# Seeding a PSUM bank by a copy so that the matmuls do the adding, in a seven-product feed-forward kernel

## The chip, the cores and the metric

The kernel runs on one core of a Trainium2 chip. The metric is device time in microseconds of one launch; the median of the runs counts, and a profile comes from one further execution. The core's engines are named as the profile names them: PE (matmuls), PEld (its weight loads), DVE, ACT and POOL, and SP, which here only issues DMAs. Each engine takes its instructions in the order in which they stand in its own program, and waits in place when an operand is not ready.

## The reference

One transformer block on 2048 tokens of width 1024: a layer norm with scale and shift from a condition vector, causal attention with a running memory in 4 segments and 32 heads, a residual, a second norm, and a gated feed-forward part of inner width 3584. The change lies in the last part:

```python
def _B_ref(x, w_gate, w_up, w_down):
    return (_gelu(x @ w_gate) * (x @ w_up)) @ w_down
...
    h = _layernorm(x, axis=-1) * (1 + cb) + sb
    x = x + gb * _B_ref(h, B_w_gate, B_w_up, B_w_down)
```

All of it is in 32-bit floats. The kernel keeps that precision by writing each operand as a high part and a low part and taking three matmuls (high-high, high-low, low-high) for each product of two 128-row tiles.

## The kernel before, in words

**The seven products.** A matrix product of 2 by 2 blocks is formed with seven block products instead of eight. The products are numbered 1 to 7, and each result block is a sum of several of them. Product 1 is the base: it is a term of all four result blocks. Products 6, 7, 5, 4 and 3 are added on top of it, and block (1,1) is product 1 plus product 2.

**Order of the work.** Attention fills the first 920 us. The projection behind it (`project`, with its DVE addition at L777) has 32 output tiles, and the last four of them, `block(3, 1)`, end at about 1125 us. Then comes the feed-forward part in three stages:

- `two(n)`, n = 0 to 13: products 1 and 2 of the outer scheme depend on the gate weights alone. They are formed here ahead of time for pairs of column chunks, with an inner scheme of seven. Index i = 1, 2 is the outer product, r the inner one, and each (i, r) is six matmuls of 128x512 (L1140). For n = 0 all r of i = 1 run before those of i = 2, and later the two alternate. `ended(i, r)` takes the bank of the product to SBUF: base r = 1 is copied by ACT to a tile `c` (L1150); for r = 6, 7, 4 DVE adds the bank `pb` and `c` (L1156); for r = 5, 3 DVE adds the bank `pc` to the result tile (L1158); r = 2 is taken from the bank `pa` by ACT (L1160) or DVE (L1162). For i = 2 POOL adds the result of i = 1 (`total`), and ACT applies the gelu (L1173). Both results go to DRAM (`st_d`).
- `gate_up(m)`, m = 0 to 55 (28 column chunks for two halves of the tokens): the outer products 6, 5, 7, 3, 4 in this order, twelve matmuls each (L1372). 6, 7 and 4 add up in the bank `pb`, 5 and 3 in the bank `pc`. The base `c1` and the finished gate half `g1` come back from DRAM. After each product DVE adds: `u2 = pb + c1` (L1384), `u3 = pc + c1` (L1387), `u3 = pb + u3` (L1390), `u2 = pc + u2` (L1393), `h2 = pb + c1` (L1397). Then ACT applies the gelu to `h2` in place (L1398) and DVE multiplies (L1399).
- `down()`: the last product, with a scheme of seven over the whole of it (L1572). The change leaves its operations alone and gives its tiles other buffers.

**What sets the order.** All engines' instructions are written out in program order in this part, by Python generators that a `step()` after each product advances: cuts of operands into high and low (`cut`: ACT writes the high part at L925, DVE or POOL subtracts at L922), loads, and the norm of the last tokens. `a_first` is the generator that prepares the token operands `AA` of `two`; `summed` in it forms sums of blocks, with one subtraction on POOL in 128x256 halves between two DVE operations. It runs beside `block(3, 1)` and the first `two`. `norm_tiles` with the name "c" transposes the last 512 tokens' tiles through a PSUM bank (L269), and ACT (L277) and DVE (L275) take them out.

**PSUM.** There are eight banks: two of tag "mm" (`pa`, and the projection's `y`), five of tag "s" (`pb`, `pc`, and much else) and one of tag "o".

Of the kernel before, what the change touches and what calls it, by code (L numbers as in the profile page):

```python
# [19 lines left out]
P = 128  # L20
# [16 lines left out]
def block_kernel(ctx: ExitStack, tc: tile.TileContext, x, c, wmod, wq, wkv, wo, beta, wg, wu, wd, out):  # L37
# [212 lines left out]
    def norm_tiles(src, dst, segs, jscale, jshift, name, tiles=range(4), wait=0, get=raw_tile, more=[]):  # L250
# [12 lines left out]
        def turn(q, h):  # L263
            t, tok = xs[q], toks[q]
            ps = s_ps(f"tp{name}{tok}_{h}")
# [608 lines left out]
    ROUND = (1, 6, 2, 7, 5, 4, 3)  # L874
# [5 lines left out]
    def feed_forward():  # L880
# [8 lines left out]
        def place(n):  # L889
            r, i = n // 8, n // 4 % 2  # L890
            at = (0 if r in (0, 2) else 1) if i == 0 else 2 if r < 4 else 3
            return ffp[at], f"A{n}"
# [8 lines left out]
        def pair_tile(name, tag, bufs, dt=F32):  # L901
            return ffp[3].tile([P, 2, HM], dt, name=name, tag=tag, bufs=bufs)
# [62 lines left out]

        def put_two(i, r, c, src, eng):
# [16 lines left out]
        def a_early():  # L983
# [7 lines left out]
            for k, r in enumerate((1, 2)):  # L991
                for c in range(2):
                    put_two(1, r, c, ts[1, c][0][:, k], nc.vector)
                    yield

# [3 lines left out]
        def a_first():  # L999

            while not normed(0, 2):
                yield
            for c in range(2):
                ts[1, c].append(unit(1, c, 1, raw_tile))
            units(0, ra_tile)
            for _ in range(3):
# [3 lines left out]
            def summed(i, c, eng=nc.gpsimd):  # L1010
# [3 lines left out]
                diff(a21, a11, a21, eng)  # L1014
# [3 lines left out]
            def put(i, r, c):  # L1018
                if r == 1:
                    put_two(i, r, c, ts[i, c][0][:, 0], nc.vector)  # L1020
                    return
                src = sums[i, c]
                if r == 3:
                    nc.vector.tensor_sub(src[3], src[2], src[6])
                put_two(i, r, c, src[r], nc.gpsimd if c and r in (5, 4) else nc.vector)

            for c in range(2):
                summed(1, c)
                yield
            for r in (6, 7, 5, 4, 3):  # L1030
                for c in range(2):
                    put(1, r, c)
                    yield
            put(2, 1, 0)
            yield
            summed(2, 0)
            yield
            for r in ROUND[1:]:
                if r == 5:
                    while (2, 1) not in ts:  # L1040
                        yield
                put(2, r, 0)
                yield
            while not ff.get("half"):
                yield
            put(2, 1, 1)
            yield
            summed(2, 1, nc.vector)
            yield
            for r in ROUND[1:]:  # L1050
                put(2, r, 1)
                yield
# [25 lines left out]
        def seven(b11, b12, b21, b22, t1, t2_, put):  # L1078
# [5 lines left out]
            yield  # L1084
            yield
# [3 lines left out]
            diff(b12, b22, b12)  # L1089
            yield  # L1090
            put(7, b12, nc.vector)
            diff(t2_, b21, t2_)
            yield
            yield
            put(5, t1, nc.vector)
            yield
            put(4, t2_, nc.vector)
            yield
            put(3, b22, nc.vector)
# [21 lines left out]
        def two(n):  # L1121

            e, o = 2 * n, 2 * n + 1
            pa, pb, pc, c, out = {}, {}, {}, {}, {}

            def product(i, r):
# [4 lines left out]
                elif r == 6:  # L1131
                    pb[i] = s_ps(f"pb{n}_{i}")
# [4 lines left out]
                for k in range(2):  # L1137
                    at = (i - 1) * 2 * P + k * P
                    for a, b in ((0, 0), (0, 1), (1, 0)):
                        nc.tensor.matmul(ps, w[:, a, at:at + P], A["a", i, r, k][b],  # L1140
                                         start=(r in (1, 6, 5) and k == a == b == 0), stop=(k == 1 and a == 1),
# [4 lines left out]
            def ended(i, r):  # L1146
                if r == 1:
                    c[i] = c_tile(f"c{n}_{i}")
                    out[i] = [pair_tile(f"{'xy'[i - 1]}{n}_{q}", "Tg"[i - 1], 5 if i == 1 else 3) for q in range(2)]
                    nc.scalar.activation(c[i], pa[i], AF.Copy)  # L1150
                    return
                z = out[i]
                q, p = {6: (1, 0), 2: (0, 0), 7: (1, 1), 5: (1, 1), 4: (0, 1), 3: (1, 0)}[r]
                t = z[q][:, p]
                if r in (6, 7, 4):
                    nc.vector.tensor_add(t, pb[i], c[i])  # L1156
                elif r in (5, 3):
                    nc.vector.tensor_add(t, pc[i], t)  # L1158
                elif i == 1:
                    nc.scalar.activation(t, pa[i], AF.Copy)  # L1160
                else:
                    nc.vector.tensor_add(t, pa[i], out[1][q][:, p])  # L1162
                if r in (6, 7):
# [7 lines left out]
                if r != 2:  # L1171
                    total(t, t, out[1][q][:, p])
                later(2, lambda: nc.scalar.activation(t, t, AF.Gelu_apprx_tanh))  # L1173
                later(4, put)

            for i, r in [(i, r) for i in (1, 2) for r in ROUND] if n == 0 else [(i, r) for r in ROUND for i in (1, 2)]:
                product(i, r)
                if n == 0 and (i, r) == (1, 4):
                    ff["half"] = True
                if n == 0 and (i, r) == (1, 3):  # L1180
                    for q in (1, 2):
                        b_two_load(q)
                    sides.append([chain(wait_for(1), b_two(1)), 1, "b"])
                if n == NJ - 1 and (i, r) == (2, 4):
# [13 lines left out]
        def a_next(p):  # L1198
# [3 lines left out]
            T_tile = lambda n: pair_tile(n, "T", 5)  # L1202
            homes = [T_tile] * 3 + [ra_tile] * 2 + [raw_tile] * 2 + [T_tile] * 3 if p == 0 else (
# [11 lines left out]
            for _ in range(5 if p else 7):  # L1215
                load()
            yield
            for q, (i, b) in enumerate(todo):
                if q > p:
                    load()  # L1220
                if p == 0 and q == 7:
# [51 lines left out]
        def w_all():  # L1273
# [25 lines left out]
            def cuts(j):  # L1299
                (e, o), (t1, t2_, t4) = rows[j], sums[j]  # L1300
                for i, src in ((6, t2_), (7, e[:, L:]), (5, t1), (4, t4)):
                    t = pair_tile(f"T{j}_{i}", "T", 5, F32R)
# [53 lines left out]
        def gate_up(m):  # L1356
# [27 lines left out]
            nc.vector.tensor_add(u2, pb, c1)  # L1384
# [576 lines left out]
```

## Time and profile before

| what | us |
|---|---|
| median of 3 runs (lowest to highest) | 2721.28 (2719.34 to 2723.15) |
| the profiled execution, own time | 2725.75 |
| its span, first to last instruction | 2724.0 |
| PE busy with matmuls in it | 2672.9 |
| DVE, ACT, POOL busy | 1752.6, 1260.2, 1066.6 |
| PE busy with the matmuls of `gate_up` (L1372) | 766.0 |
| stretch of `two`, 1125.3 to 1417.0: length, PE busy | 291.7, 280.01 |
| stretch of `gate_up`, 1417.0 to 2186.0: length, PE busy | 769.0, 765.36 |

A row of the timeline gives start, duration, engine, line, operation, result and operands, how many instructions in a row were merged, and in brackets how long the engine had been idle before and what ended that. A row of a group gives, behind the bar, the busy time in us and the mean duration in ns. Matmuls overlap: a row of PE counts each from its start to a modelled end, so a mean of 390 ns stands beside a start every 228 ns. The granted clock of TensorE (PEclk) is given as a share of full speed.

### The profile page before, as it was taken

The page shows a single profiled execution, that of the slowest core. Times are in us where ns is not written, and L with a number is a line of the kernel's source. Part 1 is how long each engine was busy: PE and PEld are TensorE (multiplying, and loading weights), DVE is VectorE, ACT ScalarE, POOL GpSimd, SP SyncE. Part 2 cuts the span into 40 slices and gives each one's busy share as a digit, 9 for nine tenths or more (in the row PEclk, how much of TensorE's full clock was granted, in tenths as well). Part 3 has the DMA queues.
Part 4 walks back from the last instruction along what each step waited for, and adds up shares of the span by engine and source line. Part 5 has one row for each costly group of instructions (what it writes and reads, how often), then busy time and mean ns, then how long its engine had stood idle before and what let it go on. Part 6 is the DMA issues. An engine that isn't in the chain of part 4 may idle for free.

```text
span 2724.0 us, 42592 instructions
## 1 busy us (share of the span) xinstructions
PE 2672.9 (98%) x14068; PEld 2223.2 (82%) x14068; DVE 1752.6 (64%) x3747; ACT 1260.2 (46%) x2924; POOL 1066.6 (39%) x1644
## 2 busy tenths in 40 slices
PE   7999999999999999899999999999999999999999
PEld 6798888888888788678877888888888888888887
DVE  6676656776777745577776655566676654575456
ACT  6778777777777634354442222232222233233323
POOL 4233334433333532365667777645665300000000
PEclk9999999999999999999999999999999999999999
DMA  7355445435443567466779988789999896785563
GB/s 263 104 158 154 120 129 149 134 112 155 115 125 105 174 228 244 143 218 212 249 268 335 333 270 270 263 304 369 374 370 374 318 339 231 264 304 201 182 208 124
DMA packets 265644, 612.32 MB, mean 225 GB/s; under 512 B 26960, under 2 KB 51536, under 8 KB 265424
## 3 DMA queue, kind: packets, MB, share of 16 engines
q1 hardware_dynamic: 265424, 609.61, 67.3%
q8 instruction: 111, 1.82, 0.3%
q14 instruction: 109, 0.89, 0.1%
HBM read 371.48 MB, written 187.70 MB: 205 GB/s over the span
## 4 chain that ended last, share of the span: by engine, by line
PE 89%; DVE 3%; DMA 2%; issue 2%; ACT 1%; POOL 1%; SPq 0%; DVEq 0%; POOLq 0%; ACTq 0%
PE f L1372 27%; PE y L1572 19%; PE kv L395 9%; PE q L401 6%; PE y L773 5%; PE pb L1140 3%; PE S L607 3%; PE T L695 3%; PE O L707 3%; PE pa L1140 2%; PE pc L1140 2%; PE kT L514 2%; PE vT L514 2%; PE num L663 1%; PE M L646 1%
## 5 line engine op out<-in xcount | busy, mean ns | idle before, releaser
L1372 PE MATMUL f<-A,B 128*128 128x512 f32 x3360 | 766.0, 390 | 3.6 <-DVE c L1390 2.1
L1372 PEld LDWEIGHTS f<-A,B 128*128 128x128 f32 x3360 | 631.5, 188 | 137.6 <-issue 4.0
L1572 PE MATMUL y<-B,L 128*128 128x512 f32 x2352 | 533.8, 389 | 0.7 <-ACT L L925 0.3
L1572 PEld LDWEIGHTS y<-B,L 128*128 128x128 f32 x2352 | 441.4, 188 | 93.0 <-ACT L L925 0.8
L611 ACT ACTIVATE sj<-sj,mm 128x384 f32<-128x384 f32 (+3 forms) x512 | 281.1, 552 | 40.0 <-DVE mm L609 39.5
L698 POOL TENSOR_SCALAR_AFFINE_SELECT pt<-pt 128x128 f32<-128x128 f32 x512 | 166.6, 347 | 331.6 <-ACT pt L697 323.8
L609 DVE CUSTOM_DVE_ANT_0 sj<-S,mask 128x384 f32<-128x384 f32 (+3 forms) x512 | 228.2, 488 | 96.5 <-PE S L607 69.4
L697 ACT ACTIVATE pt<-T 128x256 f32<-128x256 f32 (+3 forms) x512 | 182.3, 442 | 132.0 <-PE T L695 125.5
L1398 ACT ACTIVATE g<-g 128x512 f32<-128x512 f32 x56 | 35.4, 632 | 414.9 <-DVE g L1397 414.9
L925 ACT ACTIVATE L<-X 128x512 fp32r<-128x512 f32 x168 | 105.8, 630 | 256.7 <-PE y L1572 162.7
L922 DVE TENSOR_TENSOR L<-X,L 128x512 fp32r<-128x512 f32 x168 | 115.9, 691 | 145.4 <-ACT L L925 145.4
L386 POOL TENSOR_TENSOR w<-r,w 128x256 fp32r<-128x256 f32 x180 | 133.8, 774 | 141.6 <-ACT w L380 141.6
L395 PE MATMUL kv<-w,hha 128*128 128x256 f32 x896 | 173.8, 284 | 2.2 <-DVE vx L413 2.2
L1286 POOL TENSOR_TENSOR rw<-rw,gbb 128x256 f32<-128x256 f32 x112 | 107.7, 996 | 153.8 <-DMA rw<-wd 119.8
L395 PEld LDWEIGHTS kv<-w,hha 128*128 128x128 f32 x896 | 143.9, 191 | 3.4 <-DVE vx L413 2.5
L1140 PE MATMUL pb<-AA,BB 128*128 128x512 f32 x504 | 128.1, 401 | 8.1 <-DVE x L1156 4.7
L773 PE MATMUL y<-wo,hho 128*128 128x512 f32 x384 | 128.9, 399 | 2.6 <-DVE xr L777 2.6
L395 PE MATMUL kv<-w,hla 128*128 128x256 f32 x448 | 126.6, 282 | 0.0
L1140 PEld LDWEIGHTS pb<-AA,BB 128*128 128x128 f32 x504 | 96.1, 193 | 31.9 <-DVE x L1156 5.9
L695 PE MATMUL T<-qs,ks 128*128 128x256 f32 (+3 forms) x512 | 105.7, 327 | 1.8 <-DVE ry L674 1.1
L607 PE MATMUL S<-ks,qs 96*128 96x384 f32 (+3 forms) x512 | 106.8, 329 | 0.3
L925 ACT ACTIVATE B<-t 128x512 fp32r<-128x512 f32 x84 | 49.7, 623 | 118.7 <-POOL t L922 118.7
(284 smaller groups left out, 5176.3 us busy)
## 6 DMA issues: line engine op xcount, KB each, us to landing
B<-wc_d SPq DMA_DIRECT2D x112, 512.0 KB, 4.2
cg<-st_d SPq DMA_DIRECT2D x112, 256.0 KB, 6.6
hid_d<-g SPq DMA_DIRECT2D x56, 512.0 KB, 4.5
wc_d<-T SPq DMA_DIRECT2D x56, 512.0 KB, 6.8
X<-hid_d SPq DMA_DIRECT2D x112, 256.0 KB, 4.8
bc_d<-B SPq DMA_DIRECT2D x54, 512.0 KB, 5.9
B<-bc_d SPq DMA_DIRECT2D x54, 512.0 KB, 7.4
wr<-gd_d SPq DMA_DIRECT2D x84, 256.0 KB, 4.0
```

Of the source, the lines that this page charges most:

```text
L395: nc.tensor.matmul(ps, b[:, sl], w[:, a], start=(kt == 0 and a == 0 and b is hi), stop=(kt == KT - 1 and a == 1), **kw)
L401: nc.tensor.matmul(ps, w[:, a], b, start=(kt == 0 and a == 0 and b is hi), stop=(kt == KT - 1 and a == 1), **kw)
L607: nc.tensor.matmul(ps[:, :nk], qs[:96, j, i * P:(i + 1) * P], ks[:96, j, :nk], start=True, stop=True)
L609: nc.vector.tensor_tensor_reduce(out=sj[:, :nv], in0=ps[:, :nv], in1=mask[:, L - nv:], scale=-1.0, scalar=3.4e38, op0=ALU.add, op1=ALU.min ...
L611: nc.scalar.activation(sj[:, :nv], sj[:, :nv], AF.Exp, bias=mm[:, j, i:i + 1], scale=-1.0, accum_out=ll[:, i, j:j + 1])
L695: nc.tensor.matmul(ps[:, :nn], ks[:, j, kc * P:(kc + 1) * P], qs[:, j, L - nn:], start=True, stop=True)
L697: nc.scalar.activation(pt, ps[:, nn - n:nn], AF.Exp)
L698: nc.gpsimd.affine_select(pt[:, :P], pt[:, :P], pattern=[[1, P]], compare_op=ALU.is_ge, fill=0.0, base=0, channel_multiplier=-1)
L773: nc.tensor.matmul(ps, b[:, i * P:(i + 1) * P], w[:, a, g % 2], start=(g == 0 and a == 0 and b is hi), stop=(g == G - 1 and a == 1))
L1140: nc.tensor.matmul(ps, w[:, a, at:at + P], A["a", i, r, k][b], start=(r in (1, 6, 5) and k == a == b == 0), stop=(k == 1 and a == 1), skip ...
L1372: nc.tensor.matmul(ps, B[m, i][:, a, kt * P:(kt + 1) * P], A[p, i, kt][b], start=(start and kt == 0 and a == 0 and b == 0), stop=(kt == 3 ...
L1572: nc.tensor.matmul(banks[t], ops[k][:, y, t * P:(t + 1) * P], B[slots[k]][:, x], start=(i not in (2, 4, 3) and j == 0 and x == 0 and y == ...
```

## The change

- **Base through PSUM.** In `two`, ACT copies the bank `pa` of product 1 into the bank `pb` instead of into an SBUF tile, and product 6 adds onto it. In `gate_up`, ACT copies `c1` from SBUF into the bank `pb` in front of product 6, which adds onto it. The sums with the base that DVE made are then in the bank: what was a DVE addition after products 6, 5 and 4 becomes an ACT copy out of the bank, or, for product 4 of `gate_up`, the gelu read straight from the bank. DVE keeps the additions after 7 and 3.
- **Order of the seven** in `two`: 1, 5, 6, 2, 7, 3, 4 instead of 1, 6, 2, 7, 5, 4, 3; the result of i = 1 is added to that of i = 2 by DVE, and POOL's additions fall away. The cuts of the weights follow the new order.
- **Banks that accumulate.** Five matmuls, one into each "s" bank, stand in front of the first `two`, so that later matmuls add in these banks. The transposes of the late norm ("c") move to the bank of tag "o", of which there is one.
- **Operands of `two`.** `summed` makes all its differences on DVE; i = 1 and i = 2 are prepared alike, both halves of i = 2 before the first `two` has ended; the low half of a cut is written one call later than its high half (`owed`, `settle`). Tiles of tag "T" (five buffers) are split into "T" (three) and "U" (two, in another pool), and the loads of `a_next` use them.

```diff
-            ps = s_ps(f"tp{name}{tok}_{h}")
+            ps = (o_ps if name == "c" else s_ps)(f"tp{name}{tok}_{h}")
...
-    ROUND = (1, 6, 2, 7, 5, 4, 3)
+    ROUND = (1, 5, 6, 2, 7, 3, 4)
...
-            cut(hl[0], hl[1], src, eng)
-            A["a", i, r, c] = hl
+            nc.scalar.activation(hl[0], src, AF.Copy)
+            settle()
+
+            def low():
+                each(eng.tensor_sub, eng, hl[1], src, f32(hl[0]))
+                A["a", i, r, c] = hl
+
+            owed.append(low)
...
-            def summed(i, c, eng=nc.gpsimd):
+            def summed(i, c):
                 (a11, a12), (a21, a22) = ((t[:, 0], t[:, 1]) for t in ts[i, c])
                 s1 = tmp_tile(f"s1_{i}_{c}")
                 nc.vector.tensor_add(s1, a21, a22)
-                diff(a21, a11, a21, eng)
+                nc.vector.tensor_sub(a21, a11, a21)
                 nc.vector.tensor_sub(a11, s1, a11)
...
             def ended(i, r):
                 if r == 1:
-                    c[i] = c_tile(f"c{n}_{i}")
-                    out[i] = [pair_tile(f"{'xy'[i - 1]}{n}_{q}", "Tg"[i - 1], 5 if i == 1 else 3) for q in range(2)]
-                    nc.scalar.activation(c[i], pa[i], AF.Copy)
+                    pb[i] = s_ps(f"pb{n}_{i}")
+                    nc.scalar.activation(pb[i], pa[i], AF.Copy)
                     return
...
-                if r in (6, 7, 4):
-                    nc.vector.tensor_add(t, pb[i], c[i])
-                elif r in (5, 3):
-                    nc.vector.tensor_add(t, pc[i], t)
+                base = out[1][q][:, p] if i == 2 else None
+                if r == 5:
+                    nc.scalar.activation(t, pc[i], AF.Copy)
+                elif r == 6:
+                    nc.scalar.activation(t, pb[i], AF.Copy)
+                elif r in (7, 3):
+                    nc.vector.tensor_add(t, (pb if r == 7 else pc)[i], t)
+                    if base is not None:
+                        nc.vector.tensor_add(t, t, base)
...
-            g = pair_tile(f"g{m}", "g", 3)
+            g = pair_tile(f"g{m}", "g")
             h1, h2_ = (g[:, q] for q in range(2))
-            product(pb, 6, True)
-            nc.vector.tensor_add(u2, pb, c1)
+            nc.scalar.activation(pb, c1, AF.Copy)
+            product(pb, 6, False)
+            nc.scalar.activation(u2, pb, AF.Copy)
             step()
             product(pc, 5, True)
-            nc.vector.tensor_add(u3, pc, c1)
+            nc.scalar.activation(u3, pc, AF.Copy)
             step()
             product(pb, 7, False)
             nc.vector.tensor_add(u3, pb, u3)
...
             product(pb, 4, False)
-            nc.vector.tensor_add(h2_, pb, c1)
-            nc.scalar.activation(h2_, h2_, AF.Gelu_apprx_tanh)
+            nc.scalar.activation(h2_, pb, AF.Gelu_apprx_tanh)
...
+        for q in range(5):
+            nc.tensor.matmul(s_ps(f"full{q}"), B["a", 0, 1][:, 0, :P], A["a", 1, 1, 0][0], start=True, stop=True)
```

**Order on ACT between `gate_up(4)` and `gate_up(5)`.** ACT's program before, from the gelu of m = 4 to that of m = 5. `g4` and `g5` are the result tiles of m = 4 and 5, and `B6_i` the cut weights of product i for m = 6:

```order
L1398 ACTIVATE g4_17922<-g4_17922 128x512 [waits DVE_49]
L925 ACTIVATE B6_6_18083<-t1_6_18053 128x512 [waits PE_49,DMAHW6_49,Activation_49,Pool_49]
L925 ACTIVATE B6_5_18095<-t0_6_18052 128x512 [waits PE_49,Activation_49]
L925 ACTIVATE B6_7_18106<-ru6_17911 128x512 [waits PE_49,DMAHW3_49,Activation_49,Pool_49]
L925 ACTIVATE B6_3_18117<-ru6_17911 128x512 [waits DMAHW4_49,PE_49,Activation_49]
L925 ACTIVATE B6_4_18138<-t1_6_18053 128x512 [waits PE_49,Activation_49,Pool_49]
L1398 ACTIVATE g5_18040<-g5_18040 128x512 [waits DVE_49]
```

The same place now; `f0_5` is the bank `pb` of m = 5, `f1_5` its bank `pc`, `cg5_0` the base loaded from DRAM, `c0_5` and `c1_5` the tiles u2 and u3:

```order
L1401 ACTIVATE g4_17845<-f0_4_17841 128x512 [waits PE_49]
L1386 ACTIVATE f0_5_17959<-cg5_0_17715 128x512 [waits DMAHW0_49]
L1388 ACTIVATE c0_5_17961<-f0_5_17959 128x512 [waits DVE_49,PE_49]
L1391 ACTIVATE c1_5_17962<-f1_5_17960 128x512 [waits DVE_49,PE_49]
L926 ACTIVATE B6_6_18007<-t1_6_17977 128x512 [waits DMAHW6_49,Activation_49,Pool_49]
L926 ACTIVATE B6_5_18019<-t0_6_17976 128x512 [waits Activation_49]
L926 ACTIVATE B6_7_18030<-ru6_17834 128x512 [waits DMAHW3_49,Activation_49,Pool_49]
L926 ACTIVATE B6_3_18041<-ru6_17834 128x512 [waits DMAHW4_49,DVE_49]
L926 ACTIVATE B6_4_18062<-t1_6_17977 128x512 [waits Activation_49,Pool_49]
L1401 ACTIVATE g5_17963<-f0_5_17959 128x512 [waits PE_49]
```

The gelu of m = 4 now reads the bank and waits for PE, and the copy that seeds the bank for m = 5 stands directly behind it. The cuts stand behind two copies that wait for products 6 and 5 of m = 5. On PE the first matmul into `f0_5` waits for ACT. So it is at all 55 borders between one m and the next.

**Order on DVE at the start of `block(3, 1)`.** DVE's program before, up to the addition that frees the bank of tile 0 of `block(3, 1)` (`y3_1_0`); `u1_0_0`, `u1_0_1` and so on are token tiles of i = 1, and `s1` is a sum of two:

```order
L1013 TENSOR_TENSOR s1_1_0_14617<-u1_0_1_14603 128x512 [waits DMAHW4_49,DMAHW3_49,DMAHW5_49,DMAHW0_49,Activation_49]
L1015 TENSOR_TENSOR u1_0_0_14293<-s1_1_0_14617,u1_0_0_14293 128x512 [waits DVE_49,Pool_49]
L1013 TENSOR_TENSOR s1_1_1_14628<-u1_1_1_14605 128x512 [waits DMAHW5_49,DMAHW2_49]
L1015 TENSOR_TENSOR u1_1_0_14295<-s1_1_1_14628,u1_1_0_14295 128x512 [waits DVE_49,Pool_49]
L922 TENSOR_TENSOR AA1_6_0_1_14634<-u1_0_0_14293,AA1_6_0_0_14633 128x512 [waits Activation_49]
L777 TENSOR_TENSOR xr2_14586<-y3_1_0_14596,xr2_14586 128x512 [waits PE_49]
```

The same place now:

```order
L1028 TENSOR_TENSOR s1_1_0_14621<-u1_0_1_14603 128x512 [waits DMAHW4_49,DMAHW3_49,DMAHW5_49,DMAHW0_49,Activation_49]
L1029 TENSOR_TENSOR u1_0_1_14603<-u1_0_0_14286,u1_0_1_14603 128x512 [waits DVE_49]
L1030 TENSOR_TENSOR u1_0_0_14286<-s1_1_0_14621,u1_0_0_14286 128x512 [waits DVE_49]
L1028 TENSOR_TENSOR s1_1_1_14631<-u1_1_1_14605 128x512 [waits DMAHW5_49,DMAHW2_49]
L1029 TENSOR_TENSOR u1_1_1_14605<-u1_1_0_14288,u1_1_1_14605 128x512 [waits DVE_49]
L1030 TENSOR_TENSOR u1_1_0_14288<-s1_1_1_14631,u1_1_0_14288 128x512 [waits DVE_49]
L777 TENSOR_TENSOR xr2_14586<-y3_1_0_14596,xr2_14586 128x512 [waits PE_49]
```

The addition L777 had five DVE operations ahead of it, two of which waited for POOL, and has six now, none of which does.

More of the change, by code (lines that the diff above doesn't have):

```diff
@@ L999, in a_first @@
         def a_first():
-            while not normed(0, 2):
+            while not normed(0, 2) or len(ffp) < 3:
                 yield
@@ L1170, in ended @@
                     return
-                if r != 2:
-                    total(t, t, out[1][q][:, p])
                 later(2, lambda: nc.scalar.activation(t, t, AF.Gelu_apprx_tanh))
-                later(4, put)
+                later(3, put)
+            if n == 0:
+                while ("a", 1, 4, 1) not in A:
+                    next(ff["first"])
+                b_two_load(1)
             for i, r in [(i, r) for i in (1, 2) for r in ROUND] if n == 0 else [(i, r) for r in ROUND for i in (1, 2)]:
@@ L1178, in two @@
                 if n == 0 and (i, r) == (1, 4):
[L1179 to L1184, printed above, removed]
+                    b_two_load(2)
+                    sides.append([b_two(1), 1, "b"])
+                if n == NJ - 1 and (i, r) == (2, 3):
                     for q in range(2):
```

112 lines of the change are left out of this document (52 added, 60 removed).

## The prediction

> **What bounds the kernel now.** I read the page first, then the waits of PE in the stretch that the change touches, then the granted clock around the long waits. From the page, PE's share, the costliest group and the gelu:
>
> ```profile
> PE 2672.9 (98%) x14068; PEld 2223.2 (82%) x14068; DVE 1752.6 (64%) x3747; ACT 1260.2 (46%) x2924; POOL 1066.6 (39%) x1644
> ...
> L1372 PE MATMUL f<-A,B 128*128 128x512 f32 x3360 | 766.0, 390 | 3.6 <-DVE c L1390 2.1
> ...
> L1398 ACT ACTIVATE g<-g 128x512 f32<-128x512 f32 x56 | 35.4, 632 | 414.9 <-DVE g L1397 414.9
> ```
>
> PE is busy for 98% of the span. In `gate_up` it was idle for 3.6 us in all, and a matmul took 766.0/3360 = 0.228 us of it. DVE and ACT have slack: ACT's gelus waited 414.9 us for DVE, and nobody waited for them. So work taken off DVE or ACT is worth only what PE now waits for. These are all waits of PE from 1103 to 2186 us (line, what it waited for, total, times, longest):
>
> ```profile
> PE pb L1140 <- DVE x L1156: 4.7, 3, 3.3
> PE pa L1140 <- DVE xr L777: 2.9, 1, 2.9
> PE y L773 <- DVE xr L777: 2.6, 1, 2.6
> PE pb L1140 <- DVE y L1156: 2.5, 4, 1.2
> PE f L1372 <- DVE c L1390: 2.1, 1, 2.1
> PE pc L1140 <- DVE y L1158: 1.8, 1, 1.8
> PE pa L1140 <- ACT c L1150: 1.7, 2, 1.1
> PE f L1372 <- ACT B L925: 0.7, 1, 0.7
> PE pb L1140 <- ACT AA L925: 0.7, 1, 0.7
> PE f L1372 <- DVE c L1384: 0.7, 2, 0.5
> PE pb L1140 <- DVE AA L922: 0.2, 1, 0.2
> ```
>
> They sum to 20.6 us. Some of these waits cost twice, because PE ran at half the granted clock behind them (each row: stretch, length, busy us of PE, PEld, DVE, ACT, POOL, then the clock):
>
> ```profile
> 1109.40:1112.80 3.40, 3.27 (x8) 2.59 (x9) 3.40 (x6) 2.66 (x6) 1.70 (x2) 0.50 0.27 98
> 1126.50:1129.90 3.40, 3.40 (x10) 2.66 (x9) 1.27 (x2) 1.63 (x3) 0.00 (x0) 0.50 0.42 153
> 1150.70:1154.10 3.40, 3.37 (x15) 2.80 (x16) 1.18 (x2) 0.73 (x2) 3.34 (x5) 1.00 0.00 0
> 1406.40:1413.20 6.80, 5.86 (x14) 4.57 (x15) 6.80 (x12) 4.40 (x9) 2.40 (x2) 0.50 0.75 267
> 1443.90:1447.30 3.40, 3.40 (x8) 2.65 (x9) 3.37 (x5) 0.00 (x0) 3.40 (x4) 0.50 1.03 349
> ```
>
> The four stretches at 0.50 follow the waits of 2.6, 2.9, 3.3 and 2.1 us. The 1.8 us wait (third row) was followed by a clock of 1.00. Half clock for 3.4 us costs 1.7 us, so the 17.0 us at 0.50 cost 8.5. All that the change can win on these waits is 20.6 + 8.5 = 29 us, 1.1% of the time.
>
> **The change part by part: the border of `gate_up`.** ACT's instructions are in fixed order. At each of the 55 borders the gelu of m now waits for PE's last matmul of product 4, the copy that seeds the bank of m + 1 stands behind that gelu, and PE's next matmul waits for the copy. Before, PE's next matmul opened an empty bank and waited for nothing. PE now stands still for: end of matmul to start of gelu, start of gelu to start of copy, the copy, and end of copy to matmul. Rows for each, an eviction by ACT in attention, an ACT pair and a base copy in `two`, and a restart of PE behind ACT:
>
> ```profile
> 529.97 0.39 PE L514 MATMUL vT<-hhh,w 128*128 128x512 f32 x1
> ```
>
> ```profile
> 530.39 0.60 ACT L543 ACTIVATE vt<-vT 128x512 f32<-128x512 f32 x1 [0.57 <-PE vT L514]
> ```
>
> ```profile
> 1127.48 0.60 ACT L1150 ACTIVATE c<-pa 128x512 f32<-128x512 f32 x1 [3.63 <-PE pa L1140]
> 1127.97 0.62 ACT L925 ACTIVATE AA<-s 128x512 fp32r<-128x512 f32 x1
> ```
>
> ```profile
> 1160.58 0.58 ACT L1150 ACTIVATE c<-pa 128x512 f32<-128x512 f32 x1
> ```
>
> ```profile
> 1161.21 1.65 PE L1140 MATMUL pa<-AA,BB 128*128 128x512 f32 x6 [0.60 <-ACT c L1150]
> 1162.70 1.52 PE L1140 MATMUL pb<-AA,BB 128*128 128x512 f32 x6
> ```
>
> - Matmul end 530.36 to ACT's start 530.39: 0.03.
> - A bank read by ACT to the next ACT instruction: 1127.97 − 1127.48 = 0.49.
> - The copy itself, SBUF to PSUM, is not in the trace. Its nearest rows are PSUM to SBUF, 0.58 (L1150); I take 0.58. Ends: 0.49 (the rate of issue above) and 0.63 (the gelu, SBUF to SBUF).
> - Copy's end 1161.16 to the matmul at 1161.21: 0.05.
> - The idle time is thus 0.03 + 0.49 + 0.58 + 0.05 = 1.15 us. The overlap of neighbouring matmuls, 0.390 − 0.228 = 0.16, is lost on top, and six matmuls after such a wait took 1.65 against 1.52, 0.13 more.
>
> Per border 1.15 + 0.16 + 0.13 = 1.44 us, and 55 × 1.44 = **+79.2 us**. With 0.49 for the copy and no slow restart it is 1.22, 67 us. With 0.63 and one more ACT instruction (0.49 to 0.53) at half of the borders it is about 1.76, 97 us. I see no row by which it could be nothing, since PE has no other work in its order between the two products.
>
> [...]
>
> **The rest of `gate_up`.** Three of DVE's seven operations per m become ACT's, or go. The evictions of 6 and 5 by ACT have cover: bank `pb` is next written by product 7, after twelve matmuls of product 5 (2.7 us), against 0.6 for the copy. ACT's cuts of weights now stand behind them. ACT's order at a border before:
>
> ```profile
> 1598.95 0.63 ACT L1398 ACTIVATE g<-g 128x512 f32<-128x512 f32 x1 [5.59 <-DVE g L1397]
> ...
> 1606.32 0.64 ACT L925 ACTIVATE B<-t 128x512 fp32r<-128x512 f32 x1 [4.65 <-POOL t L922]
> 1612.55 0.63 ACT L1398 ACTIVATE g<-g 128x512 f32<-128x512 f32 x1 [5.59 <-DVE g L1397]
> ```
>
> The last cut before a gelu waits for POOL and ended 5.6 us before the gelu; the eviction of 5 starts some 7 us after the gelu, so the cuts begin about 7 us later than now, and that last cut may come close to the gelu. I take 0, and make it a rival. PE's 2.1 us wait at 1443.83 stays: DVE's addition L1390 stood behind an operation that waited for a load, which the change does not touch:
>
> ```profile
> 1441.87 1.21 DVE L959 TENSOR_TENSOR m<-rm,rm 128x512 f32<-128x512 f32 x1 [4.10 <-DMA rm<-h_d]
> ```
>
> So 0, with a bound of −(2.1 + 1.7) = −3.8. The very first copy (m = 0) comes behind the end of `two`: +1.0, from 0 to 3 (the longest wait of that place now, 3.3).
>
> **`two`.** The waits on what the change takes off DVE and POOL are 4.7 + 2.5 + 1.8 + 1.7 = 10.7 us, and with half clock at 1406 (6.8/2 = 3.4) 14.1. Banks of 6 and 5 must still be emptied, by ACT, which has gelus and cuts in its order there, and DVE still adds to the bank sums of 7 and 3. I take −6, under half, between −14.1 and as much again as the waits now, +10.7. The copy from `pa` to `pb` costs nothing: product 5 of the same index, six matmuls and 1.52 us, lies between product 1 and product 6, against 0.03 + 0.58 + 0.05. If another ACT wait stood ahead of it, that is the +10.7.
>
> **`block(3, 1)` and the start of `two`.** DVE before:
>
> ```profile
> 1104.60 0.69 DVE L1015 TENSOR_TENSOR u<-s,u 128x512 f32<-128x512 f32 x1 [1.60 <-POOL u L922]
> ...
> 1107.58 0.69 DVE L1015 TENSOR_TENSOR u<-s,u 128x512 f32<-128x512 f32 x1 [1.69 <-POOL u L922]
> ```
>
> 1.60 + 1.69 = 3.3 us of waiting for POOL goes, against PE's 2.6 us wait for the L777 that stands behind these two; DVE gains one operation (0.69) and has one cut fewer ahead. So the first wait goes with its half clock: −(2.6 + 1.7) = −4.3. The second (2.9 us, at the first `two`) I let shrink below the length that brought half clock: −1.7. Together −6, from 0 to −(2.6 + 2.9 + 2 × 1.7) = −8.9. The five extra matmuls stand where PE waits for L777: 5 × 0.228 = 1.1 if uncovered, I take +0.5.
>
> **The late transposes.** In the one bank "o", the second group of four waits until ACT has emptied the first:
>
> ```profile
> 1196.82 0.60 PE L269 MATMUL tpc<-ident,nc 128*128 128x128 f32 x4
> ...
> 1198.65 0.60 PE L269 MATMUL tpc<-ident,nc 128*128 128x128 f32 x4
> ```
>
> ```profile
> 1199.41 1.49 ACT L277 ACTIVATE htc<-tpc,modT 128x128 f32<-128x128 f32 x4
> ```
>
> ACT could begin at 1197.45 and end at 1198.94; PE restarts at 1198.99 instead of 1198.65: 0.34, with the restart 0.47, four tiles, **+1.9**. Ends: 0, and 6.0 if all of 1.49 is waited for each time.
>
> **The sum.** 79.2 + 1.0 − 6 − 6 + 0.5 + 1.9 = +70.6 us. Against the profiled execution, 2725.75 + 70.6 = 2796.3. The median of the runs lies 4.5 below that execution (2721.28), so **2792 us**.
>
> **The rivals.**
>
> - *Faster: the border is nearly free.* If the copy came ahead of the wait, or the gelu's bank were handed over early, only the gains would be left. With the whole 29 us the point of decision is 29/55 = 0.53 us per border, with my gains (70.6 − 79.2 = −8.6) 0.16; all gains and no border give 2721 − 29 = 2692. For it: ACT has 54% of its time free. Against it: the order on ACT is fixed, and even a single ACT instruction between two matmuls costs 0.6 (the row at 1161.21). That the sums don't move to PE as said is part of this. 3%.
> - *Half clock at each border.* 55 × 1.7 = 94 us more: 2886. Against it, 1.15 us is well under the 1.8 us that left the clock at 1.00. For it, the waits here come every 14 us, which no stretch of before shows. [...] The trace so far speaks against it by the third window above; no row has waits as frequent. 4%.
> - *The gelu late behind the cuts.* If the last cut ends 1 us after product 4 in the 27 borders where it waits for POOL (m below 28), 27 × 1.0 more: 2819. For it, the cuts begin 7 us later; against it, the 5.6 us to spare, and POOL's differences are its own and need not begin later. 8%.
> - *My forecast*: 85%.
>
> **How the numbers follow.** The terms' ends summed give 67 − 14.1 − 8.9 − 3.8 = +40 and 97 + 3 + 10.7 + 1.1 + 6 = +118, that is 2761 to 2839. All at one end at once is unlikely, so I cut the upper end by the +10.7 of `two` and some of the rest, and the lower by some 10 us: 2770 to 2820, which takes in the late gelu at 2819 and leaves out the free border and the half clock (7%) and what lies in the cut ends. About 0.2% is what a measurement of this kernel can tell from no change. Faster by more than that: 2%, from the first rival; within it 1%, the same rival with a border of some 0.2 to 0.3 us; slower 97%.
>
> **What would show it.** In the trace after, the matmuls of `gate_up` should have about 55 waits on ACT's copy L1386, each 1.1 to 1.3 us long, some 64 us in all; a gelu starting within 0.1 us of product 4's end; and a granted clock that stays at 1.00 behind them. In `two`, waits on DVE x and y additions should be shorter; at 1109 us PE should not wait for L777. The prediction is wrong if the waits on L1386 are few or under 0.5 us, if the clock shows 0.50 at the borders, or if gelus wait for cuts and not for PE.

## The result and the profile after

| what | before | after |
|---|---|---|
| median, us | 2721.20 | 2817.78 |
| lowest to highest, us | 2719.34 to 2723.15 | 2816.52 to 2818.70 |
| ratio, 95% interval | | 1.0355 [1.0337, 1.0372] |
| profiled execution, own time | 2725.75 | 2816.52 |

The change made the kernel slower by 96.6 us by the medians, and by 90.8 us between the two profiled executions. The forecast was +70.6. Of the 5.8 us between the two figures, 4.5 are the distance of the profiled execution before from its median, and 1.3 that of the one after. Sign and cause were right, the border of `gate_up` came out as worked out, and the gain that I had expected in front of it was a loss.

The page after, PE's share, the group of `gate_up`'s matmuls (its line is now L1375) and the gelu:

```profile
PE 2691.4 (96%) x14073; PEld 2218.8 (79%) x14073; DVE 1652.6 (59%) x3540; ACT 1384.8 (49%) x3162; POOL 1013.9 (36%) x1554
...
L1375 PE MATMUL f<-A,B 128*128 128x512 f32 x3360 | 781.0, 392 | 70.7 <-ACT f L1386 70.7
...
L1401 ACT ACTIVATE g<-f 128x512 f32<-128x512 f32 x56 | 33.4, 597 | 231.1 <-PE f L1375 231.1
```

DVE lost 100 us of work and PE stood still longer. In front of the matmuls of `gate_up` the idle time went from 3.6 us to 70.7, all of it for ACT's copy L1386, and their busy time from 766.0 to 781.0. The gelus now wait for PE. All waits of PE from the late projection to the end of `gate_up` (total, times, longest):

```profile
PE f L1375 <- ACT f L1386: 70.7, 56, 5.8
PE pb L1139 <- DVE y L1160: 8.1, 12, 0.9
PE tpc L269 <- ACT htc L277: 7.0, 4, 2.4
PE pb L1139 <- DVE x L1160: 5.4, 4, 2.9
PE y L773 <- DVE xr L777: 2.4, 2, 1.5
PE pa L1139 <- DVE xr L777: 1.9, 1, 1.9
PE tpc L269 <- ACT nc L248: 0.9, 2, 0.6
```

One border, on ACT and then on PE (start, length, what it is; in brackets the idle time before it):

```profile
1461.62 0.60 ACT L1401 ACTIVATE g<-f 128x512 f32<-128x512 f32 x1 [2.00 <-PE f L1375]
1462.11 0.60 ACT L1386 ACTIVATE f<-cg 128x512 f32<-128x512 f32 x1
1465.81 0.60 ACT L1388 ACTIVATE c<-f 128x512 f32<-128x512 f32 x1 [3.10 <-PE f L1375]
```

```profile
1447.69 13.89 PE L1375 MATMUL f<-A,B 128*128 128x512 f32 x60 [1.18 <-ACT f L1386]
1462.76 13.89 PE L1375 MATMUL f<-A,B 128*128 128x512 f32 x60 [1.18 <-ACT f L1386]
```

PE's matmuls end at 1447.69 + 13.89 = 1461.58, the gelu starts 0.04 later, the copy 0.49 behind the gelu, the copy ends at 1462.71 and PE goes on 0.05 later: 1.18 us, against the 1.15 of the forecast. It is the same at all 55 borders: 70.7 − 5.8 = 64.9 us over 55.

By stages, `two` and then `gate_up`, before and after (length, then busy us of PE, PEld, DVE, ACT and POOL, the clock, the DMA share, GB/s):

```profile
1125.40:1415.70 290.30, 278.70 (x1209) 226.16 (x1210) 209.84 (x329) 136.34 (x240) 170.21 (x204) 0.98 0.66 222
1415.70:2185.70 770.00, 766.36 (x3365) 632.26 (x3364) 494.41 (x655) 200.16 (x358) 479.72 (x553) 1.00 0.91 327
```

```profile
1119.70:1430.90 311.20, 283.93 (x1209) 226.15 (x1209) 191.01 (x289) 174.42 (x314) 115.32 (x130) 0.97 0.61 207
1430.90:2277.20 846.30, 781.39 (x3364) 628.65 (x3365) 409.57 (x483) 285.86 (x521) 484.63 (x542) 1.00 0.84 295
```

`gate_up` lost 76.3 us, `two` 20.9. The projection's second half took 211.3 us instead of 213.0 (−1.7), `down` 0.7 less, and everything ahead of the projection 4.0 less: together 76.3 + 20.9 − 1.7 − 0.7 − 4.0 = 90.8. The 4.0 are no part of the change: in the kernels below that projection starts at 906.4 to 912.3 us with the same instructions ahead of it. That is the scatter of one profiled execution against another.

The granted clock behind the longest transpose wait (0.53), behind the very first copy (0.50), and behind a border (1.00):

```profile
1216.00:1219.40 3.40, 3.27 (x10) 2.78 (x11) 1.96 (x5) 1.08 (x3) 0.00 (x0) 0.53 0.99 325
...
1430.80:1434.20 3.40, 3.32 (x8) 2.68 (x9) 0.00 (x0) 0.57 (x2) 0.00 (x0) 0.50 0.99 278
...
1477.80:1481.20 3.40, 3.37 (x15) 2.79 (x16) 0.40 (x1) 0.32 (x1) 3.08 (x4) 1.00 1.03 386
```

None of the 55 borders brought half clock: from 1434.67 to 2813.65 us, with all of them, the clock record stands at 1.00.

**Where `two` lost.** PE's idle time in `two` went from 11.6 us (290.30 − 278.70) to 27.3 (311.20 − 283.93), and its busy time grew by 5.2. The waits for additions, copies and cuts, 11.6 us before, didn't shrink: the additions alone take 13.5 now (8.1 and 5.4). The transposes (7.0 and 0.9) and the first copy (5.8) are new. So there are three places. The first is in 12 of the 14 n, at product 4: DVE's addition behind product 7 of i = 2 stood behind the low half of the cut of the next weight. ACT, DVE and PE around it:

```profile
1276.17 0.63 ACT L926 ACTIVATE BB<-t_a 128x512 fp32r<-128x512 f32 x1 [1.57 <-PE pc L1139]
```

```profile
1276.84 0.69 DVE L923 TENSOR_TENSOR BB<-t_a,BB 128x512 fp32r<-128x512 f32 x1 [0.76 <-ACT BB L926]
1277.45 0.68 DVE L1160 TENSOR_TENSOR y<-pb,y 128x512 f32<-128x512 f32 x1
```

```profile
1273.19 2.88 PE L1139 MATMUL pc<-AA,BB 128*128 128x512 f32 x12
1275.91 1.52 PE L1139 MATMUL pb<-AA,BB 128*128 128x512 f32 x6
1278.18 1.65 PE L1139 MATMUL pb<-AA,BB 128*128 128x512 f32 x6 [0.75 <-DVE y L1160]
```

The bank was full when product 7 ended, at about 1273.4, but DVE stood and waited for ACT's cut, and ACT's cut waited for PE's product 3 (until 1276.1). Three engines in a ring; PE waits 0.75 us.

The second place is the transposes. PE, then ACT:

```profile
1211.69 0.66 PE L269 MATMUL tpc<-ident,nc 128*128 128x128 f32 x4
...
1216.13 1.08 PE L269 MATMUL tpc<-ident,nc 128*128 128x128 f32 x4 [2.40 <-ACT htc L277]
```

```profile
1212.54 0.58 ACT L1148 ACTIVATE pb<-pa 128x512 f32<-128x512 f32 x1
1213.05 0.61 ACT L1175 ACTIVATE y<-y 128x512 f32<-128x512 f32 x1
1213.57 0.61 ACT L926 ACTIVATE BB<-g 128x512 fp32r<-128x512 f32 x1
1214.09 0.58 ACT L1148 ACTIVATE pb<-pa 128x512 f32<-128x512 f32 x1
1214.60 1.48 ACT L277 ACTIVATE htc<-tpc,modT 128x128 f32<-128x128 f32 x4
```

ACT could have emptied the bank from 1212.4 on and began at 1214.60, because two copies `pb<-pa`, a gelu and a cut stood ahead of it.

The third is the first seeding copy. DVE, ACT and PE at the end of `two`:

```profile
1428.27 0.68 DVE L1160 TENSOR_TENSOR y<-pc,y 128x512 f32<-128x512 f32 x1
1428.98 0.69 DVE L1162 TENSOR_TENSOR y<-y,x 128x512 f32<-128x512 f32 x1
```

```profile
1429.71 0.63 ACT L1175 ACTIVATE y<-y 128x512 f32<-128x512 f32 x1 [3.78 <-DVE y L1162]
1430.24 0.58 ACT L1386 ACTIVATE f<-cg 128x512 f32<-128x512 f32 x1
```

```profile
1430.88 1.65 PE L1375 MATMUL f<-A,B 128*128 128x512 f32 x3 [5.81 <-ACT f L1386]
```

The copy stood behind a gelu of the last `two`, which waited 3.78 us for DVE, and PE waited 5.81 us for the copy. Where PE opens `gate_up` without the base, the same backlog on DVE doesn't hold it up (experiment 1).

### The profile page after: what moved, and what is told of

The parts are those of the page before. It is cut to its first block, busy times and chain, and to the rows that moved or that the text cites. A ratio compares the mean times of both kernels' runs of the same rounds, so it can differ in the third digit from the quotient of the medians.

```text
span 2814.8 us, 42379 instructions
## 1 busy us (share of the span) xinstructions
PE 2691.4 (96%) x14073; PEld 2218.8 (79%) x14073; DVE 1652.6 (59%) x3540; ACT 1384.8 (49%) x3162; POOL 1013.9 (36%) x1554
## 3 DMA queue, kind: packets, MB, share of 16 engines
q8 instruction: 111, 1.82, 0.3%
## 4 chain that ended last, share of the span: by engine, by line
PE 83%; DMA 5%; DVE 5%; ACT 4%; issue 2%; SPq 1%; POOL 1%; ACTq 0%; DVEq 0%; POOLq 0%
PE f L1375 24%; PE y L1575 18%; PE kv L395 9%; PE q L401 6%; PE y L773 4%; PE S L607 3%; PE O L707 3%; PE T L695 3%; PE pb L1139 3%; PE pc L1139 2%; PE pa L1139 2%; PE vT L514 1%; ACT f L1386 1%; PE kT L514 1%; DMA B<-bc_d 1%
## 5 line engine op out<-in xcount | busy, mean ns | idle before, releaser
L1375 PE MATMUL f<-A,B 128*128 128x512 f32 x3360 | 781.0, 392 | 70.7 <-ACT f L1386 70.7
L1375 PEld LDWEIGHTS f<-A,B 128*128 128x128 f32 x3360 | 627.7, 188 | 223.7 <-ACT f L1386 94.4
L923 DVE TENSOR_TENSOR B<-t,B 128x512 fp32r<-128x512 f32 x56 | 52.4, 936 | 164.3 <-ACT B L926 164.3
L1401 ACT ACTIVATE g<-f 128x512 f32<-128x512 f32 x56 | 33.4, 597 | 231.1 <-PE f L1375 231.1
L923 DVE TENSOR_TENSOR B<-ag,B 128x512 fp32r<-128x512 f32 x81 | 71.7, 886 | 122.7 <-ACT B L926 122.7
L1388 ACT ACTIVATE c<-f 128x512 f32<-128x512 f32 x56 | 33.5, 598 | 168.5 <-PE f L1375 168.5
```

Of the source, the lines that this page charges most:

```text
L923: f(*xs)
L1375: nc.tensor.matmul(ps, B[m, i][:, a, kt * P:(kt + 1) * P], A[p, i, kt][b], start=(start and kt == 0 and a == 0 and b == 0), stop=(kt == 3 ...
```

## Experiments

Ratios are against the kernel before on the same chip, with 95% intervals.

**1. The sums of `gate_up` back on DVE.** All else of the change stays.

```diff
-            nc.scalar.activation(pb, c1, AF.Copy)
-            product(pb, 6, False)
-            nc.scalar.activation(u2, pb, AF.Copy)
+            product(pb, 6, True)
+            nc.vector.tensor_add(u2, pb, c1)
...
-            nc.scalar.activation(u3, pc, AF.Copy)
+            nc.vector.tensor_add(u3, pc, c1)
...
-            nc.scalar.activation(h2_, pb, AF.Gelu_apprx_tanh)
+            nc.vector.tensor_add(h2_, pb, c1)
+            nc.scalar.activation(h2_, h2_, AF.Gelu_apprx_tanh)
```

> The changed kernel with gate_up as it was before: product 6 opens an empty bank, DVE adds the base, the gelu works in place. Everything else of the change stays. Theory (PE waits at the border for ACT's copy, and nothing else in gate_up changed): gate_up falls back by about 76 us to some 770 us, and the first copy's wait of 5.8 us goes or shrinks, so 2817.8 - 76 - (0 to 6) = 2736 to 2742 us; 15 to 21 us of the loss then belong to the stage of two. Rival (the loss is spread over the kernel, or the relief of DVE in gate_up is worth something): the time stays over 2755, or falls below 2725.

2730.16 us, 1.0025 [1.0015, 1.0035]. `gate_up` in its profile:

```profile
1422.60:2188.40 765.80, 765.48 (x3365) 632.34 (x3364) 493.19 (x657) 197.93 (x356) 475.12 (x545) 1.00 0.92 328
```

The theory holds, with some 6 us more than it gave. `gate_up` is 80.5 us shorter than in the changed kernel, and 4.2 shorter than before: PE's wait of 2.1 us for L1390 and its half clock are gone here too, which I had said would stay. The first copy's 5.8 us are gone. What is left of the loss is in `two`.

**2. The copy ahead of the gelu.** The same instructions, two of them in the other order on ACT.

```diff
             product(pb, 4, False)
+            if m + 1 < NCH:
+                seed(m + 1)
             nc.scalar.activation(h2_, pb, AF.Gelu_apprx_tanh)
```

> The changed kernel with two ACT instructions per border in the other order: the copy that seeds the bank of m + 1 stands directly ahead of the gelu of m. The work is the same, instruction for instruction. Theory (the order on ACT makes PE wait): the 55 waits of 1.18 us go, and with them the 15 us by which PE's busy time in gate_up grew; 55 x (1.18 + 0.27) = 80 us less, 2733 to 2742 us. Rival A (a bank filled by ACT, or ACT beside PE in PSUM, makes the matmuls themselves slower): the waits go but the 15 us stay, 2750 to 2756 us. Rival B (ACT has too much to do and the gelu or the copy comes late anyway): PE waits for ACT at many borders still, over 2760 us.

2734.09 us, 1.0043 [1.0029, 1.0057], as the theory had it, and some 16 us or more below what either rival gave. So 3.1% of the time hung on the order of two ACT instructions, and not on the amount of work or on where the sum is made. Rivals A and B are out by the time; that an early copy leaves no waits at the borders is shown in experiment 8.

**3. The transposes in the "s" banks.**

```diff
-            ps = (o_ps if name == "c" else s_ps)(f"tp{name}{tok}_{h}")
+            ps = s_ps(f"tp{name}{tok}_{h}")
...
-                nc.tensor.transpose(ps[:, k * P:(k + 1) * P], t[:, kt * P:(kt + 1) * P], ident)
+                nc.tensor.matmul(ps[:, k * P:(k + 1) * P], t[:, kt * P:(kt + 1) * P], ident, is_transpose=True,
+                                 start=k == 0, stop=k == 3, skip_group_check=True)
```

> The changed kernel with the late norm's transposes in the five s banks, as before (the first of four opens the bank, the other three don't). Theory (the single o bank made PE wait for ACT): the 7.0 us of waits on L277 go, and the half clock behind two of them, 2 x 1.7: 2806 to 2811 us. Rival (the s banks are then short, and the products of two wait for a bank instead): 2814 to 2820 us.

2811.27 us, 1.0327 [1.0312, 1.0343]: about 7 us better, just at the theory's edge. `two` is 3.6 us shorter in its profile. Its waits for the transposes' evacuation:

```profile
PE tpc L269 <- ACT htc L278: 1.9, 1, 1.9
PE pc L1140 <- ACT htc L278: 1.9, 1, 1.9
```

7.0 us became 3.8; half of the rival was true, as one product of `two` now waits for such a bank. The waits on DVE's x additions were 8.5 us in this execution, where the changed kernel had 5.4.

**4. DVE's addition ahead of the cut.** One step of the side work is put off behind product 7 of i = 2.

```diff
                 ended(i, r)
-                step()
+                if (i, r) != (1, 7) or n == 0:
+                    step()
+                if (i, r) == (2, 7) and n:
+                    step()
```

> The changed kernel with one step of the side work in each two put off, so that DVE's addition behind product 7 of i = 2 stands ahead of the low half of the next weight's cut and not behind it. Theory (PE's 12 waits of about 0.7 us at product 4 come from DVE waiting in front of that addition for a cut by ACT, which waits for PE): 8.1 us of waits and 12 restarts of 0.13 to 0.29 go, 2806 to 2810 us. Rival (the cut that is put off makes the weights late, and PE waits for them): 2815 us or more.

2802.66 us, 1.0296 [1.0278, 1.0313], some 15 us better, more than the theory's 8 to 12. PE and DVE at the place shown above (here some 8 us earlier):

```profile
1264.86 2.88 PE L1139 MATMUL pc<-AA,BB 128*128 128x512 f32 x12
1267.58 2.88 PE L1139 MATMUL pb<-AA,BB 128*128 128x512 f32 x12
```

```profile
1267.07 0.67 DVE L1160 TENSOR_TENSOR y<-pb,y 128x512 f32<-128x512 f32 x1
```

Product 4 of both indices runs through. The twelve waits on y are gone, and `two` takes 296.1 us, 15.1 less. Of that, 5.1 us are three stretches at half clock (1.7 us each) that the changed kernel had at 1120.6, 1216.2 and 1243.5 us and that did not come in this execution (its mean granted clock is 0.997, against 0.995 in the changed kernel), though the waits ahead of them are as long: 1.86, 2.39 and 1.88 us. My estimate is that this hangs on where the waits fell in time and not on the edit: the last section shows it for one wait of 1.82 us, and for these three it isn't shown. The other 10 us are what the theory gave. Whether the other three executions went without these stretches too isn't shown.

**5. Two copies at the border.** The seeding copy is issued twice.

```diff
             nc.scalar.activation(pb, c1, AF.Copy)
+            nc.scalar.activation(pb, c1, AF.Copy)
             product(pb, 6, False)
```

> The changed kernel with the seeding copy at each border issued twice, one behind the other into the same bank. Theory (PE stands and waits for what ACT does there, at ACT's rate of one such instruction each 0.49 to 0.58 us): 56 x 0.49 to 0.58 = 27 to 32 us more, 2845 to 2850 us, the waits 1.7 us each; half clock at the borders, if it comes at 1.7 us already, would show here first, with up to 94 us more. Rival (the border is set by something else, a semaphore's way or PE's restart): under 10 us more.

2926.31 us, 1.0745 [1.0731, 1.0759]: 108 us more than the changed kernel, not 27 to 32. The borders' waits, three borders on PE, and the clock behind the first and the third:

```profile
PE f L1375 <- ACT f L1387: 99.7, 55, 1.8
```

```profile
1503.23 15.50 PE L1375 MATMUL f<-A,B 128*128 128x512 f32 x60 [1.81 <-ACT f L1387]
1520.55 15.49 PE L1375 MATMUL f<-A,B 128*128 128x512 f32 x60 [1.81 <-ACT f L1387]
1537.85 13.89 PE L1375 MATMUL f<-A,B 128*128 128x512 f32 x60 [1.81 <-ACT f L1387]
```

```profile
1503.70:1507.10 3.40, 3.40 (x10) 2.62 (x9) 1.59 (x2) 0.00 (x0) 2.87 (x3) 0.50 0.85 288
1538.00:1541.40 3.40, 3.40 (x16) 2.79 (x17) 1.91 (x2) 0.49 (x1) 3.19 (x4) 1.00 0.99 242
```

The second copy itself cost 99.7 − 64.9 = 34.8 us, 0.63 a border: the theory's price, a little above its upper end. Half clock followed 45 of the 55 borders (the whole stage has a mean clock of 0.92), and 45 × 1.7 = 77 us. Together that is 112, a little more than the 109 by which `gate_up` grew in the profile (955.4 − 846.3). The rival of the prediction that I had given 4% was one ACT instruction away.

**6. A copy and a bit.** 16 of the 512 columns are copied a second time.

```diff
             nc.scalar.activation(pb, c1, AF.Copy)
+            nc.scalar.activation(pb[:, :16], c1[:, :16], AF.Copy)
```

> The changed kernel with one short ACT instruction more at each border, a copy of 16 of the 512 columns behind the whole copy; a 128x16 ACT instruction of attention took 0.215 us. The waits should grow from 1.18 us to 1.35 to 1.45. In the changed kernel 0 of 55 borders brought half clock at 1.18 us, in the kernel with two whole copies 45 of 55 at 1.81. Theory (a stretch of 3.41 us on a grid of its own, in which PE stands for more than about 1.2 us, is followed by one at half clock; 45 of 55 fits an idle share that starts there, if waits fall anywhere on the grid): some 36 to 40 of 55 borders at 1.4 us, 55 x 0.22 + 38 x 1.7 = 77 us more, 2880 to 2905 us. Rival (it takes 1.5 us or more): no or few half-clock stretches, 10 to 16 us more, 2828 to 2836 us.

2830.87 us, 1.0403 [1.0385, 1.0420]. The waits:

```profile
PE f L1375 <- ACT f L1387: 76.9, 55, 1.4
```

76.9/55 = 1.40 us each, 12 us more in all, and no stretch at half clock behind them (the mean clock of the profiled execution is 0.995, as in the changed kernel). The theory of a point at 1.2 us fell, the rival holds: with one wait per border, half clock came behind none of 55 at 1.40 us and behind 45 of 55 at 1.81 (the last section says more).

**7. The edits in `two`, without the seeding of `gate_up`.** Edits 1, 3 and 4 together.

> The three edits that helped in two, without the seeding in gate_up: gate_up adds on DVE as before, the transposes go through the s banks, DVE's addition behind product 7 stands ahead of the cut. Theory (the parts are independent and add up): ratio 1.0025 - 0.0059 - 0.0023 = 0.994, 2707 us beside a kernel before of 2723, faster than both. Rival (the waits only move on): 1.000 or more.

2717.13 us, 0.9974 [0.9965, 0.9982]: faster than both kernels, but by 0.26% and not 0.6%. In the profile `two` took 286.2 us against 305.7 in experiment 1, which is near edit 4 (15.1) and edit 3 (3.6) together. The projection began at 912.3 us in this execution and at 906.4 in that of experiment 1, 6 us of scatter ahead of everything that the edits touch. A sum over four ratios, each with an interval of about 0.001 to 0.002 on either side, is not sure to better than 0.003, which is the size of the miss; a cause for it isn't shown.

**8. The edits in `two`, with the copy issued early.** As 7, but `gate_up` is seeded, the copy for m + 1 stands ahead of product 7 of m, and m = 0 is summed as before.

```diff
+            if m + 1 < NCH:
+                seed(m + 1)
             product(pb, 7, False)
...
-            product(pb, 6, False)
+            product(pb, 6, m == 0)
```

> The same two edits in two, but with the seeding in gate_up, the copy for m + 1 issued ahead of product 7 of m, and m = 0 not seeded at all (its base is added by DVE as before). Theory (seeding is neither good nor bad once no PE instruction waits for the copy, since PE is the bound and DVE's relief is worth nothing there): no wait on the copy, gate_up at 764 to 768 us, ratio 0.993 to 0.995, the same as the kernel that sums on DVE within 0.1 %. Rival A (DVE's relief is worth something): faster than that one by over 0.15 %. Rival B (ACT beside PE in the same memory slows the matmuls): gate_up at 775 us or more, ratio over 1.000.

2717.76 us, 0.9978 [0.9969, 0.9987]. PE's waits in `gate_up`, and the stage:

```profile
PE f L1383 <- DVE c L1409: 0.6, 4, 0.2
PE f L1383 <- DVE c L1398: 0.2, 1, 0.2
```

```profile
1413.40:2179.20 765.80, 764.92 (x3366) 631.04 (x3365) 418.23 (x493) 286.84 (x521) 492.21 (x547) 1.00 0.92 328
```

No wait on the copy, and the same length to the tenth as with the sums on DVE (experiment 1), though DVE has 418 us of work here instead of 493. In kernel 7 itself `gate_up` took 768.2 us and `two` 286.2, here 765.8 and 290.0: the two differ by a few us each way, and the medians by 0.6. The ratio missed its forecast as in 7; against kernel 7 it is the same, which was the theory. Rivals A and B are out: DVE's relief is worth nothing clear of noise, and ACT in PSUM costs PE nothing that shows.

**9. The last `two`.** As 8, with DVE's additions of n = 13 ahead of the cuts for `gate_up`.

```diff
+                late = {(2, 2): 1, (1, 7): 1, (1, 3): 1} if n == NJ - 1 else {(1, 7): 1} if n else {}
+                held[0] += 1
+                if (i, r) not in late:
+                    while held[0]:
+                        held[0] -= 1
+                        step()
```

> As the kernel with the early copy, and in the last two (n = 13) the steps of the side work that cut the token operands of gate_up are put behind DVE's additions after products 7 and 3. Theory (DVE's cuts in front of those additions make PE wait 2.9 to 3.2 us at product 4 and bring half clock): 3 us of waiting and 1.7 to 3.4 us of half clock less, ratio 0.991 to 0.993. Rival (the cuts are needed for the first products of gate_up and PE waits for them instead): no gain, or slower.

2715.79 us, 0.9975 [0.9966, 0.9984], no different from 8: the theory fell. PE now waited at the other end of the same place:

```profile
PE f L1385 <- DVE x L1161: 3.1, 1, 3.1
```

The wait at product 4 of the last n fell from 2.94 us in experiment 8 to 1.74, and 3.1 us of waiting for DVE came up in `gate_up`, near what the rival said. That the amount of DVE's work there sets the wait, and not its order, fits this, but no run took work away.

## Why the prediction was right or wrong

- **The border**: forecast +79.2, measured 64.9 of idle time and 781.0 − 766.0 = 15.0 of busy time lost to overlap and restart, 79.9 together. Each piece was right: 0.04, 0.49, 0.60 for the copy (0.58 taken, 0.597 in the mean), 0.05. Experiment 2 shows the cause.
- **The rest of `gate_up`**: forecast 0, with −3.8 as a bound. The stage grew by 76.3, 3.6 less than the border: the waits of before in it are gone. Experiments 1 and 8 show it without the border.
- **The late gelu** didn't come. The last cut of a period ended 2.00 us before the gelu at 1461.62 (ACT's idle time there), where it had 5.6 before, and all 231.1 us of idle time in front of the gelus ended with PE.
- **The projection**: forecast −6, and +0.5 for the five extra matmuls; measured −1.7. The half clock at 1109 us went as forecast, and that is the 1.7. The waits didn't go: the one of 2.6 us became two, of 0.81 and 1.55, and the one of 2.9 became 1.87 because the five extra matmuls fill a part of it. From the end of the projection's last matmul (1116.72) to the first of `two` (1119.72) it is 3.0 us. POOL's waits went, as I had worked out, but DVE then had the cuts and differences of i = 2 in front of later L777s, which I had not followed.
- **`two`, the step that failed**: with the transposes and the first copy I had −6 + 1.9 + 1.0 = −3.1, and it was +20.9. I took "−6, under half", as if the waits on L1156 and L1158 were prices of the additions. They are waits for a place in DVE's queue, and the additions that remain kept theirs, behind the cut: 10.7 us of waits were to shrink, and they are 13.5 (experiment 4 wins 10 us there, and 5 of half clock besides). For the transposes I let ACT begin at once, and it had four instructions ahead (1.9 forecast, 7.0 waited, plus half clock). And the first copy was priced without what it stood behind (1.0 forecast, 5.8 waited).
- **Half clock at each border** didn't come, and the reason I gave, that 1.15 us is under the 1.8 that left the clock alone, was weaker than it looked: at 1.81 us it came 45 times in 55 (experiment 5). The single wait of 1.82 us before was no proof that such waits are safe (the last section says what spared it).
- **Luck in the time**: 2817.78 lies 2.2 us under the upper end of the range. I had taken the +10.7 of `two` out of that end, and `two` alone came out 24.0 above its terms (20.9 + 3.1); the late gelu at 2819, which that end was to take in, didn't come. The border was worked out; that the whole still fell inside was luck.

## What to carry to other kernels

When an engine must write a bank before PE may use it, look at what stands ahead of that write in the engine's own order: if it waits for PE's last matmul, the round trip is paid at each group, here 1.18 us at each of 55 borders, and moving the write ahead of that instruction gave it all back here (experiment 2, 2817.78 to 2734.09 us). In this kernel, work taken from an engine that PE doesn't wait for was worth nothing clear of noise (experiment 8: 418 us of DVE's work in `gate_up` instead of 493, and the same 765.8 us), and the place of the remaining work in that engine's queue was worth some 10 us (experiment 4), though moving it didn't help everywhere (experiment 9). Price a step that moves to another engine by what stands ahead of it there, not by its own length.

## What was not expected of the hardware

- PE's waits had a cliff in these runs. Waits of 1.18 us (the changed kernel) and of 1.40 us (experiment 6) at each of 55 borders never brought half clock; at 1.81 us (experiment 5) 45 of 55 did, and the matmuls of such a border then took 15.5 us instead of 13.89, so that 0.41 us more of waiting mostly cost 1.6 us on top of itself. Between 900 and 2700 us of the two kernels' profiles the half-clock stretches each last 3.413 us or twice that, and their starts lie on a grid of that step: before at 1109.39, 1126.46, 1406.35 and 1443.90 us, which are 5, 82 and 11 times 3.413 apart, and in the changed kernel at 1120.64, 1216.21, 1243.52, 1421.01 and 1427.84, which are 28, 8, 52 and 2 times 3.413 apart. In experiment 5, eight borders of the timeline from 1500 to 1640 us can be laid on such a grid, by estimate, from the half-clock row at 1503.70. Seven waits ended 0.2 to 1.3 us ahead of a line, and the 60 matmuls behind them took 15.48 to 15.53 us; the eighth, the third in the rows of experiment 5, ended within 0.05 us of a line (1537.85), and those behind it took 13.89, at full clock. Why the other nine borders stayed at full clock isn't shown.
- PE's idle time within one stretch of that grid fits better than the length of a wait. I added it up for each stretch of 3.413 us from 900 us on, in the profiles of the two kernels. The nine stretches at full clock with 1.87 us or more of it (before 2.09 to 2.47, after 1.87 to 2.77) were all followed by one at half clock, and none with 1.75 us or less was. The wait of 1.82 us before, from 1148.91 to 1150.73, was split by the line at 1150.35 into 1.43 and 0.38, and the clock stayed at 1.00; waits of 1.81 us in experiment 5 mostly brought half clock, so the length alone doesn't tell. A stretch already at half clock was followed by another with 0.99 us of idle time (before, 1406.35) and with 3.04 (after, 1427.84), and by none with 0.18 or less.
- A copy by ACT took 0.597 us from SBUF to PSUM (L1386, x55), 0.581 from PSUM to PSUM (L1148, x28), 0.598 from PSUM to SBUF (L1388, x56), all in the changed kernel. The base copy of `two` took 0.584 to SBUF before (x28) and 0.581 to PSUM now: where it writes made hardly a difference here, at 128x512.
